# Sums across the 32-partition groups: one fp32 matmul, or a rounded part and a rest in one fp32r matmul

## The chip, the cores and the metric

The kernel runs on one core of a Trainium2 chip, in one launch. The metric is device time in microseconds (us). PE is the matrix engine, PEld its weight load, DVE the vector engine, ACT the scalar engine, POOL the GpSimd engine, SP the engine that issues most DMAs. SBUF is the on-chip memory of 128 partitions, PSUM the memory that PE writes.

## The reference

A transformer block with adaptive layer norms, cut to what matters:

```python
mod = (silu(c) @ w_mod).reshape(1, 6, 1, 576)        # sa, ca, ga, sb, cb, gb
h = layernorm(x) * (1 + ca) + sa                     # x: 1 x 2048 x 576
x = x + ga * A(h)
h = layernorm(x) * (1 + cb) + sb
x = x + gb * B(h)

def A(x):                                            # attention, 32 heads of 128, 16 key/value heads
    q = x @ wq
    k, v = last 512 rows of k_cache, v_cache
    p = softmax(q @ k.T * 128 ** -0.5)               # over 512 keys
    return (p @ v) @ wo

def B(x):                                            # feed-forward, 4608 wide
    return (relu(x @ W_gate) * (x @ W_up)) @ W_down
```

All inputs and the output are fp32. The softmax of A needs, for each query, a maximum over 512 keys and a sum over 512 keys.

## The kernel before, in words

Attention is done in 128 units. A unit is one head and one block of 512 queries, and takes the keys as rows: the scores of a unit stand in PSUM as keys x queries, in two halves of 2 x 128 keys (`s_half`, tiles `s`). So maximum and sum over the keys go across the partitions.

Almost all matrix products are in fp32r, the reduced fp32 form that PE takes in one pass. To keep the precision, an operand is split into a rounded part `hi` (an fp32r copy) and the rest `lo` (value minus `hi`), and a product is three matmuls: hi by hi, hi by lo, lo by hi. ACT makes the `hi` copies and POOL the `lo` subtractions. In a unit POOL does two additions for the sum over the keys (`ks`, L548), two subtractions `lo` for the probabilities (L539, 128 x 1024 each), one for the output (`olo`, L573), and in many units one for a weight (L182) or for a later stage (L818, L855, L863, L865).

The maximum of a unit goes in three steps. DVE takes the maxima of blocks of 32 partitions, with a transpose inside (L460, tile `t4`). `max_pre` takes the maximum over the four key tiles (L468, into PSUM) and multiplies it by `mask` (L469), so that each group of 32 partitions ("quadrant") holds its own values in its own of four column groups of 16, and zeros in the others. Then `spread` on PE multiplies these 64 columns by `quad`, a 128 x 128 matrix of ones where two partitions have the same place in their quadrant. That copies the four quadrants' values to all partitions. `max_bc` takes the maximum of the four (L498) and transposes it back to rows (L513). The sum of the unit before rides along: `sum_pre` writes the 32-blocks' sums into 16 more columns (L475, tile `t5`), the same matmul adds the four quadrants, and `sum_inv` takes the reciprocal (L488). The matmul (L483) has thus 80 columns, is in fp32, and shows as two records a time in the profile.

The order of the engines is written out by hand: Tile is told to keep the program's order on PE, DVE, ACT and POOL, and each engine runs its own queue in that order. For unit u it is:

- `s_half` twice, `max_pre(u)`, `sum_pre(u - 1)`
- `qproj(u + 1)`: 14 matmuls on PE for the next unit's queries (L383)
- `spread(u)`, `max_bc(u)`
- a piece of the output projection, 12 matmuls of 288 columns (L584)
- `pv_half(u - 1, 0)`: probabilities by values (L557 to L559)
- `exp_half(u, 0)` and `(u, 1)`: DVE subtracts the maximum (L530), ACT takes the exponential (L532) and the `hi` copy (L519)
- the rest of `pv`, another piece, and at the end `lo_half` twice on POOL (L539)

Between these lie the steps of a schedule (weights' loads and splits, layer norms, preparations for the next stage), each due at a time in tenths of a unit. In the first four units and the last (`by_pe`) the maximum is subtracted on PE; there `max_bc` splits the maxima with an fp32r copy `rh` on DVE (L505 to L508). After the last unit a `spread` with the last sums alone runs inside the feed-forward stage (`last_unit`).

Of the kernel before, what the change touches and what calls it, by code (L numbers as in the profile page):

```python
# [33 lines left out]
def kernel(  # L34
# [13 lines left out]
    nc = tc.nc  # L48
# [3 lines left out]
    cp = ctx.enter_context(tc.tile_pool(name="cp", bufs=1))  # L52
# [7 lines left out]
    op = ctx.enter_context(tc.tile_pool(name="op", bufs=3))  # L60
# [13 lines left out]
    mhalf = cp.tile([P, 4], F32, name="mhalf")  # L74
# [11 lines left out]
    mask = cp.tile([P, 4], F32, name="mask")  # L86
# [8 lines left out]
    nc.vector.tensor_scalar(minus, intc, 0.0, -1.0, op0=ALU.is_equal, op1=ALU.mult)  # L95


    cT = cp.tile([P, 5], F32, name="cT")
    nc.sync.dma_start(cT, c)
    acc = []  # L100
    accp = [res.tile([P, 2, D], F32, tag=f"accp{i}", name=f"acc{i}") for i in range(S // (2 * P))]
# [5 lines left out]
            nc.sync.dma_start(acc[i], x[i * P:(i + 1) * P, :])  # L107


    sT = cp.tile([P, 5], F32, name="sT")  # L110
# [5 lines left out]
    msum = {}  # L116

    steps_done = {}

# [43 lines left out]
    def mod_col(j, plus):  # L163
        m = msum[j]
        assert steps_done[j] == (3 if j == 1 else 5)
        if j < 3:
            mod_pad(j)
        ps = psM.tile([P, 512], F32, tag="mm", name=f"mps{j}")
        for t in range(5):
            nc.tensor.matmul(ps[:, t:t + 1], m[:, t * P:(t + 1) * P], ones[:, 0:1], start=True, stop=True)  # L170
        r = cp.tile([P, 5], F32, name=f"mcol{j}")
# [236 lines left out]
    NU = HKV * NQB * 2  # L408
# [33 lines left out]
    st_, t4, t5, pt, hi_, lo_, bc, rb, rinv, ks_, pvps, done, o, bps = ({} for _ in range(14))  # L442

    def by_pe(u):
        return u < PE0 or u >= NU - PE1
# [16 lines left out]
                                axis=AX.X, op=ALU.max, apply_transpose=True)  # L462

    def max_pre(u):
        t5[u] = sp.tile([P, 5, 16], F32, tag="t5", name=f"t5_{u}", bufs=1)
        bps[u] = psM.tile([P, 512], F32, tag="mm", name=f"qm{u}")
        t = bps[u][:, 128:144]
        nc.vector.tensor_reduce(t, t4.pop(u).rearrange("p k b -> p b k"), axis=AX.X, op=ALU.max)  # L468
        nc.vector.tensor_tensor(t5[u][:, 0:4, :], mask[:, :, None].to_broadcast([P, 4, 16]),  # L469
                                t[:, None, :].to_broadcast([P, 4, 16]), op=ALU.mult)  # L470

    def sum_pre(u):
        if u + 1 == NU:
            t5[NU] = sp.tile([P, 5, 16], F32, tag="t5", name=f"t5_{NU}", bufs=1)
        nc.vector.tensor_reduce(t5[u + 1][:, 4, :],  # L475
                                ks_.pop(u).rearrange("p (b j) -> p b j", j=32),
                                axis=AX.X, op=ALU.add, apply_transpose=True)

    def spread(u):
        a, b = (0 if u < NU else 4), (5 if u else 4)  # L480
        if u == NU:
            bps[u] = psM.tile([P, 512], F32, tag="mm", name=f"qm{u}")
        nc.tensor.matmul(bps[u][:, a * 16:b * 16], quad,  # L483
                         t5.pop(u)[:, a:b, :].rearrange("p a b -> p (a b)"), start=True, stop=True)

    def sum_inv(u):
        r = rinv[u] = sp.tile([P, 16], F32, tag="ri", name=f"ri{u}", bufs=1)
        nc.vector.reciprocal(r, bps[u + 1][:, 64:80])  # L488

    def sum_bc(u):  # L490
        r = rinv.pop(u)
# [2 lines left out]
                            r[:, :, None].to_broadcast([P, 16, 32]))  # L494

    def max_bc(u):
        r = sp.tile([P, 16], F32, tag="r", name=f"r{u}", bufs=1)
        nc.vector.tensor_reduce(r, bps[u][:, :64].rearrange("p (a b) -> p b a", a=4), axis=AX.X, op=ALU.max)  # L498
        if u:
            sum_inv(u - 1)  # L500
        m = bp.tile([P, 512], F32, tag="bc", name=f"mb{u}")
        if by_pe(u):
            rh = sp.tile([P, 16], F32R, tag="rh", name=f"rh{u}", bufs=1)
            rr = sp.tile([P, 16, 2], F32, tag="rr", name=f"rr{u}", bufs=1)
            nc.vector.tensor_copy(rh, r)  # L505
# [657 lines left out]
    e = 10 * NU  # L1163
# [460 lines left out]
```

## Time and profile before

| | |
|---|---|
| runs, median | 2932.51 us (2930.28 to 2934.88, 3 runs) |
| the profiled execution | 2927.97 us, its span 2926.2 us, mean granted PE clock 0.996 |
| PE busy | 2854.1 us, 98% of the span |
| DVE busy | 2220.3 us, 76% |
| POOL busy | 2110.1 us, 72% |
| ACT busy | 1432.2 us, 49% |
| first and last crossing matmul (L483) | at 42.3 us and at 1651.8 us |

In a row of the profile stand the line of the kernel, the engine, the operation, the tile written and those read, the shapes, and the count; then the busy time and the mean length of one in ns, and the idle time of the engine in front of them with what ended it. A timeline's row has the start, the length, the engine, the line, and the count of like instructions that are merged in it; in square brackets stands the idle time in front and what ended it. In a line's own view the three numbers are the shortest, the median and the longest in ns, and then the first and the last start in us. In the table by stretches stand the length, the busy times of PE, PEld, DVE, ACT and POOL with their counts, the granted clock, the DMA share and GB/s.

### The profile page before, as it was taken

How to read it: one execution, taken by the hardware profiler on the slowest of the kernel's cores; microseconds unless marked ns; L12 is line 12 of the kernel's file. 1: busy time of each engine (PE TensorE's matmuls, PEld its weight loads, DVE VectorE, ACT ScalarE, POOL GpSimd, SP SyncE). 2: the span in 40 equal slices, each digit the busy share in tenths (PEclk: the TensorE clock that was granted, in tenths of full speed). 3: DMA queues.
4: the chain of work that ended last, by engine and by line, in shares of the span. 5: the costliest groups of instructions: out<-in, count | busy, mean ns of one | idle time of the engine just before them, and what ended most of it. 6: DMA issues, size and time to landing. Idle time of an engine off the chain costs nothing. (4 is left out here: it accounts for less than half of the span.)

```text
span 2926.2 us, 41388 instructions
## 1 busy us (share of the span) xinstructions
PE 2854.1 (98%) x15214; PEld 2483.7 (85%) x15214; DVE 2220.3 (76%) x3082; ACT 1432.2 (49%) x2029; POOL 2110.1 (72%) x1564
## 2 busy tenths in 40 slices
PE   6799999999999999999999999999999999999999
PEld 5588888888888888888888788888888888888888
DVE  7878888788878888777889677677777466666666
ACT  4566666666666666666656343333333122222221
POOL 5588888888888889876778666777777356656553
PEclk9999999999999999999999999999999999999999
DMA  4011222222223223322244456666666944444442
GB/s 151 22 45 55 82 94 84 67 98 93 92 83 107 90 63 133 101 70 85 65 145 135 135 214 223 229 230 222 225 227 243 331 160 153 151 152 153 158 151 104
DMA packets 162698, 396.44 MB, mean 135 GB/s; under 512 B 14912, under 2 KB 61760, under 8 KB 162496
## 3 DMA queue, kind: packets, MB, share of 16 engines
q1 hardware_dynamic: 131472, 282.15, 29.9%
q10 hardware_dynamic: 31024, 111.65, 9.8%
q8 instruction: 120, 1.97, 0.3%
q14 instruction: 82, 0.67, 0.1%
HBM read 268.73 MB, written 153.32 MB: 144 GB/s over the span
## 5 line engine op out<-in xcount | busy, mean ns | idle before, releaser
L539 POOL TENSOR_TENSOR lo<-p,hi 128x1024 fp32r<-128x1024 f32 x256 | 609.7, 2403 | 1.1 <-ACT hi L519 1.1
L548 POOL TENSOR_TENSOR ks<-ks,p 128x512 f32<-128x512 f32 x256 | 343.7, 1343 | 271.1 <-ACT p L532 206.6
L460 DVE TRANSPOSE_TENSOR_REDUCE t<-s 128x32 f32<-128x1024 f32 x256 | 316.7, 1243 | 137.4 <-PE s L457 125.9
L929 PE MATMUL gu<-hop_B,wop 128*128 128x512 f32 (+1 forms) x1512 | 378.2, 393 | 0.0
L929 PE MATMUL gu<-hop_T,wop 128*128 128x512 f32 (+1 forms) x1260 | 320.5, 394 | 1.9 <-DMA wop<-wk_P 1.9
L383 PE MATMUL qps<-hTa,wA 128*128 128x512 f32 x1288 | 311.7, 393 | 9.4 <-ACT lfa L365 8.9
L929 PEld LDWEIGHTS gu<-hop_B,wop 128*128 128x128 f32 (+1 forms) x1512 | 275.8, 188 | 52.1 <-ACT lflh L914 0.9
L584 PE MATMUL wo<-woga,ohi 128*128 128x288 f32 x1472 | 305.9, 301 | 1.5 <-DVE lfa L363 1.5
L383 PEld LDWEIGHTS qps<-hTa,wA 128*128 128x128 f32 x1288 | 244.2, 190 | 61.7 <-ACT lfa L365 8.2
L530 DVE TENSOR_TENSOR p<-s,mb 128x1024 f32<-128x1024 f32 x246 | 290.1, 1218 | 4.1
L519 ACT CAST hi<-p 128x1024 fp32r<-128x1024 f32 x256 | 268.9, 1050 | 7.1
L584 PE MATMUL md<-wogb,hhi 128*128 128x288 f32 x1280 | 261.8, 297 | 9.6 <-DVE acc L595 8.7
L929 PEld LDWEIGHTS gu<-hop_T,wop 128*128 128x128 f32 (+1 forms) x1260 | 228.1, 188 | 43.8 <-DMA wop<-wk_P 2.1
L532 ACT ACTIVATE p<-p 128x1024 f32<-128x1024 f32 x246 | 259.9, 1056 | 8.0 <-DVE p L530 7.9
L584 PEld LDWEIGHTS wo<-woga,ohi 128*128 128x128 f32 x1472 | 238.7, 188 | 9.1 <-issue 1.9
L435 ACT ACTIVATE qhi<-qps 128x512 fp32r<-128x512 f32 x128 | 76.5, 597 | 340.8 <-PE qps L383 340.8
L595 DVE TENSOR_TENSOR acc<-md,acc 128x576 f32<-128x576 f32 x160 | 120.5, 754 | 152.6 <-PE md L584 151.5
L584 PEld LDWEIGHTS md<-wogb,hhi 128*128 128x128 f32 x1280 | 212.8, 188 | 24.8 <-DVE acc L595 12.7
L1039 DVE TENSOR_TENSOR acc<-st_P,acc 128x576 f32<-128x576 f32 x160 | 120.9, 756 | 133.8 <-PE st_P L1030 133.8
L584 PE MATMUL wo<-woga,olo 128*128 128x288 f32 x736 | 216.9, 295 | 0.3 <-POOL olo L573 0.2
L584 PE MATMUL md<-wogb,hlo 128*128 128x288 f32 x640 | 188.9, 295 | 0.0
L573 POOL TENSOR_TENSOR olo<-rb,ohi 128x512 fp32r<-128x512 f32 x128 | 166.6, 1302 | 23.7 <-ACT ohi L569 23.2
(249 smaller groups left out, 7093.2 us busy)
## 6 DMA issues: line engine op xcount, KB each, us to landing
wop<-wk_P SPq DMA_DIRECT2D x133, 640.0 KB
wk_P<-wop ACTq DMA_DIRECT2D x119, 640.0 KB
wr<-wlay SPq DMA_DIRECT2D x68, 384.0 KB
rogb<-wd SPq DMA_DIRECT2D x68, 288.0 KB
againq<-akq SPq DMA_DIRECT2D x18, 640.0 KB
rwA<-wq SPq DMA_DIRECT2D x32, 320.0 KB
wlay<-wg SPq DMA_DIRECT2D x36, 256.0 KB
roga<-wo SPq DMA_DIRECT2D x32, 288.0 KB
```

The lines of the kernel that those rows point to most:

```text
L383: return [lambda i=i, a=a, b=b: nc.tensor.matmul(ps, a, b, start=(i == 0), stop=(i == n - 1)) for i, (a, b) in enumerate(ops)]
L460: nc.vector.tensor_reduce(t4[u][:, 2 * h:2 * h + 2, :].rearrange("p k b -> p (k b)"), t.rearrange("p k (b j) -> p (k b) j", j=32), axis=AX ...
L519: nc.scalar.copy(hi_[u, h], pt[u, h])
L530: nc.vector.tensor_tensor(p, t, bc[u][:, None, :].to_broadcast([P, 2, 512]), op=ALU.subtract)
L532: nc.scalar.activation(p, p, AF.Exp, bias=0.0, scale=1.0)
L539: nc.gpsimd.tensor_sub(lo_[u, h], pt[u, h], hi_[u, h].bitcast(F32))
L548: nc.gpsimd.tensor_tensor(ks_[u], ks_[u], p[:, j, :], op=ALU.add)
L573: nc.gpsimd.tensor_sub(olo[u], o.pop(u), ohi[u].bitcast(F32))
L584: nc.tensor.matmul(ps[:, half, :H2], a[:, sl], w[b][:, cs], start=(n == 0 and seed is None), stop=(n == 5), skip_group_check=seed is not None)
L595: nc.vector.tensor_tensor(av, ps[:, :, :H2], av, op=ALU.add)
L929: nc.tensor.matmul(ps, a, c, start=s not in ("P2", "P3") and i == 0, stop=i == len(ops) - 1, skip_group_check=True)
L1039: nc.vector.tensor_tensor(t, ps[:, :, :H2], t, op=ALU.add)
```

## The change

The 80 columns are no longer multiplied in fp32. `max_pre` and `sum_pre` write a tile `te`. A new step `cut(u)`, after them and before `qproj(u + 1)`, makes on DVE a rounded fp32r copy of it and the rest (value minus copy), side by side in `t5`. `spread` multiplies both, 160 columns, by `quad` (now fp32r) in one fp32r matmul. A new step `spread_add` on DVE adds the two halves again in PSUM, then takes the maximum of the four quadrants and the reciprocal; the maximum now stays in PSUM. In a unit that makes one copy, one subtraction and one reduce more on DVE. To make room, small constants share one tile `small`, and some tags are shared.

```diff
-    quad = cp.tile([P, P], F32, name="quad")
+    quad = cp.tile([P, P], F32R, name="quad")
...
     def max_pre(u):
-        t5[u] = sp.tile([P, 5, 16], F32, tag="t5", name=f"t5_{u}", bufs=1)
         bps[u] = psM.tile([P, 512], F32, tag="mm", name=f"qm{u}")
-        t = bps[u][:, 128:144]
+        t = bps[u][:, 160:176]
         nc.vector.tensor_reduce(t, t4.pop(u).rearrange("p k b -> p b k"), axis=AX.X, op=ALU.max)
-        nc.vector.tensor_tensor(t5[u][:, 0:4, :], mask[:, :, None].to_broadcast([P, 4, 16]),
+        te[u] = sp.tile([P, 5, 16], F32, tag="t4", name=f"te{u}", bufs=1)
+        nc.vector.tensor_tensor(te[u][:, 0:4, :], mask[:, :, None].to_broadcast([P, 4, 16]),
                                 t[:, None, :].to_broadcast([P, 4, 16]), op=ALU.mult)
...
+    def groups(u):
+        return 0 if u < NU else 4, 5 if u else 4
+
+    def cut(u):
+        a, b = groups(u)
+        e = te.pop(u)[:, a:b, :]
+        t5[u] = sp.tile([P, 2, 5, 16], F32R, tag="t5", name=f"t5_{u}", bufs=1)
+        hi, lo = (t5[u][:, i, a:b, :] for i in range(2))
+        nc.vector.tensor_copy(hi, e)
+        nc.vector.tensor_sub(lo, e, hi.bitcast(F32))
+
     def spread(u):
-        a, b = (0 if u < NU else 4), (5 if u else 4)
+        a, b = groups(u)
         if u == NU:
             bps[u] = psM.tile([P, 512], F32, tag="mm", name=f"qm{u}")
-        nc.tensor.matmul(bps[u][:, a * 16:b * 16], quad,
-                         t5.pop(u)[:, a:b, :].rearrange("p a b -> p (a b)"), start=True, stop=True)
-
-    def sum_inv(u):
-        r = rinv[u] = sp.tile([P, 16], F32, tag="ri", name=f"ri{u}", bufs=1)
-        nc.vector.reciprocal(r, bps[u + 1][:, 64:80])
+        n = (b - a) * 16
+        nc.tensor.matmul(bps[u][:, :2 * n].rearrange("p (s n) -> p s n", s=2), quad,
+                         t5.pop(u)[:, :, a:b, :].rearrange("p s a b -> p s (a b)"), start=True, stop=True)
+
+    def spread_add(u):
+        a, b = groups(u)
+        n = (b - a) * 16
+        sx = bps[u][:, 176:176 + n]
+        nc.vector.tensor_reduce(sx, bps[u][:, :2 * n].rearrange("p (s n) -> p n s", s=2), axis=AX.X, op=ALU.add)
+        if u < NU:
+            r = bps[u][:, 256:272]
+            nc.vector.tensor_reduce(r, sx[:, :64].rearrange("p (a b) -> p b a", a=4), axis=AX.X, op=ALU.max)
+        if u:
+            ri = rinv[u - 1] = sp.tile([P, 16], F32, tag="ri", name=f"ri{u - 1}", bufs=1)
+            nc.vector.reciprocal(ri, sx[:, n - 16:])
+        return r if u < NU else None
...
     def max_bc(u):
-        r = sp.tile([P, 16], F32, tag="r", name=f"r{u}", bufs=1)
-        nc.vector.tensor_reduce(r, bps[u][:, :64].rearrange("p (a b) -> p b a", a=4), axis=AX.X, op=ALU.max)
-        if u:
-            sum_inv(u - 1)
+        r = spread_add(u)
...
     def last_unit():
+        cut(NU)
         spread(NU)
-        sum_inv(NU - 1)
+        spread_add(NU)
...
         max_pre(u)
         if u:
             sum_pre(u - 1)
+        cut(u)
         run(u, 1)
         if u + 1 < NU:
             qproj(u + 1, 0, 14)
```

More of the change, by code (lines that the diff above doesn't have):

```diff
@@ L73 @@
     nc.vector.tensor_scalar(ident, ident, 0.0, None, op0=ALU.is_equal)
-    mhalf = cp.tile([P, 4], F32, name="mhalf")
+    small = cp.tile([P, 33], F32, name="small")
+    mhalf, mask, sT = small[:, :4], small[:, 4:8], small[:, 8:13]
     nc.vector.memset(mhalf, -0.5)
@@ L85 @@
     inta = bp.tile([P, 4], I32, tag="bc", name="inta")
-    mask = cp.tile([P, 4], F32, name="mask")
     nc.gpsimd.iota(inta, pattern=[[-32, 4]], base=0, channel_multiplier=1)
@@ L95 @@
     nc.vector.tensor_scalar(minus, intc, 0.0, -1.0, op0=ALU.is_equal, op1=ALU.mult)
-    cT = cp.tile([P, 5], F32, name="cT")
+    cT = sp.tile([P, 5], F32, tag="t4", name="cT", bufs=1)
     nc.sync.dma_start(cT, c)
@@ L107, in load_x @@
             nc.sync.dma_start(acc[i], x[i * P:(i + 1) * P, :])
-    sT = cp.tile([P, 5], F32, name="sT")
     nc.scalar.activation(sT, cT, AF.Exp, bias=0.0, scale=-1.0)
@@ L114 @@
     nc.vector.tensor_tensor(sT, sT, cT, op=ALU.mult)
-    msum = {}
+    msum, cols = {}, []
     steps_done = {}
@@ L170, in mod_col @@
             nc.tensor.matmul(ps[:, t:t + 1], m[:, t * P:(t + 1) * P], ones[:, 0:1], start=True, stop=True)
-        r = cp.tile([P, 5], F32, name=f"mcol{j}")
+        r = small[:, 13 + 5 * len(cols):18 + 5 * len(cols)]
+        cols.append(j)
         def done():
@@ L440, in q_lo @@
                                        op0=ALU.mult, op1=ALU.subtract)
-    st_, t4, t5, pt, hi_, lo_, bc, rb, rinv, ks_, pvps, done, o, bps = ({} for _ in range(14))
+    te, st_, t4, t5, pt, hi_, lo_, bc, rb, rinv, ks_, pvps, done, o, bps = ({} for _ in range(15))
     def by_pe(u):
@@ L473, in sum_pre @@
         if u + 1 == NU:
-            t5[NU] = sp.tile([P, 5, 16], F32, tag="t5", name=f"t5_{NU}", bufs=1)
-        nc.vector.tensor_reduce(t5[u + 1][:, 4, :],
-                                ks_.pop(u).rearrange("p (b j) -> p b j", j=32),
+            te[NU] = sp.tile([P, 5, 16], F32, tag="t4", name=f"te{NU}", bufs=1)
+        nc.vector.tensor_reduce(te[u + 1][:, 4, :], ks_.pop(u).rearrange("p (b j) -> p b j", j=32),
                                 axis=AX.X, op=ALU.add, apply_transpose=True)
+    def groups(u):
[7 more added lines that the diff above has]
+        nc.vector.tensor_sub(lo, e, hi.bitcast(F32))
     def spread(u):
-        a, b = (0 if u < NU else 4), (5 if u else 4)
+        a, b = groups(u)
         if u == NU:
             bps[u] = psM.tile([P, 512], F32, tag="mm", name=f"qm{u}")
-        nc.tensor.matmul(bps[u][:, a * 16:b * 16], quad,
-                         t5.pop(u)[:, a:b, :].rearrange("p a b -> p (a b)"), start=True, stop=True)
-    def sum_inv(u):
-        r = rinv[u] = sp.tile([P, 16], F32, tag="ri", name=f"ri{u}", bufs=1)
-        nc.vector.reciprocal(r, bps[u + 1][:, 64:80])
+        n = (b - a) * 16
[13 more added lines that the diff above has]
+        return r if u < NU else None
     def sum_bc(u):
@@ L496, in max_bc @@
     def max_bc(u):
-        r = sp.tile([P, 16], F32, tag="r", name=f"r{u}", bufs=1)
-        nc.vector.tensor_reduce(r, bps[u][:, :64].rearrange("p (a b) -> p b a", a=4), axis=AX.X, op=ALU.max)
-        if u:
-            sum_inv(u - 1)
+        r = spread_add(u)
         m = bp.tile([P, 512], F32, tag="bc", name=f"mb{u}")
         if by_pe(u):
-            rh = sp.tile([P, 16], F32R, tag="rh", name=f"rh{u}", bufs=1)
-            rr = sp.tile([P, 16, 2], F32, tag="rr", name=f"rr{u}", bufs=1)
+            rh = sp.tile([P, 16], F32R, tag="t5", name=f"rh{u}", bufs=1)
+            rr = sp.tile([P, 16, 2], F32, tag="t4", name=f"rr{u}", bufs=1)
             nc.vector.tensor_copy(rh, r)
```

## Prediction

> **What bounds the kernel now.** I read the page's totals first, then who waits around the matmul that the change replaces, then the order of time of one attention unit, then POOL's rows.
>
> ```profile
> span 2926.2 us, 41388 instructions
> PE 2854.1 (98%) x15214; PEld 2483.7 (85%) x15214; DVE 2220.3 (76%) x3082; ACT 1432.2 (49%) x2029; POOL 2110.1 (72%) x1564
> L539 POOL TENSOR_TENSOR lo<-p,hi 128x1024 fp32r<-128x1024 f32 x256 | 609.7, 2403 | 1.1 <-ACT hi L519 1.1
> ```
>
> PE is busy for 98% of the span, so PE's stream is the limit and anything that holds it back costs in full. The source view of the crossing (L483) says how close it is to doing that already:
>
> ```profile
> L483 PE MATMUL qm<-t,quad x258: 180/272/337, 42.3 to 1651.8; 128*128 128x80 f32 x127, 128*128 128x64 f32 x1, 128*128 128x16 f32 x1
>   DVE t L475: 17.2, 22
> ```
>
> Each of the 129 crossings is two matmul records. PE waited for DVE's operand before 22 of them only, 17.2 us in all; in the others the operand lay ready. Here is that place in one unit, from the timelines of all engines, of DVE and of ACT:
>
> ```profile
> 1256.66 0.22 DVE L498 TENSOR_REDUCE r<-qm 128x16 f32<-128x64 f32 x1 [0.93 <-PE qm L483]
> 1257.66 2.35 DVE L530 TENSOR_TENSOR p<-s,mb 128x1024 f32<-128x1024 f32 x2
> 1258.36 0.64 ACT L593 COPY acc<-wo 128x576 f32<-128x576 f32 x1
> 1259.61 1.05 ACT L532 ACTIVATE p<-p 128x1024 f32<-128x1024 f32 x1
> ...
> 1265.40 4.75 POOL L539 TENSOR_TENSOR lo<-p,hi 128x1024 fp32r<-128x1024 f32 x2
> 1266.31 2.21 PE L383 MATMUL qps<-hTa,againq 128*128 128x512 f32 x9
> 1266.66 0.28 DVE L468 TENSOR_REDUCE qm<-t 128x16 f32<-128x64 f32 x1
> 1266.97 0.22 DVE L469 TENSOR_TENSOR t<-mask,qm 128x64 f32<-128x64 f32 x1
> 1267.11 0.70 DVE L475 TRANSPOSE_TENSOR_REDUCE t<-ks 128x16 f32<-128x512 f32 x1
> 1268.35 0.35 PE L483 MATMUL qm<-t,quad 128*128 128x80 f32 x2
> 1268.50 0.52 PE L584 MATMUL wo<-againo,ohi 128*128 128x288 f32 x2
> 1268.74 0.22 DVE L498 TENSOR_REDUCE r<-qm 128x16 f32<-128x64 f32 x1 [0.93 <-PE qm L483]
> 1268.86 0.29 PE L584 MATMUL wo<-againo,olo 128*128 128x288 f32 x1
> 1268.99 0.43 PE L584 MATMUL wo<-againo,ohi 128*128 128x288 f32 x2
> 1269.25 0.29 PE L584 MATMUL wo<-againo,olo 128*128 128x288 f32 x1
> ```
>
> The operand is complete at 1267.81 and PE comes to it at 1268.35: 0.54 us of slack. L498 to L498 is 12.08 us, one unit. At 1267.81 POOL is inside its two `lo` subtractions, which last until 1270.15. That decides this change.
>
> **The PE part.** Nine 512-column matmuls run from 1266.31 to 1268.35, 0.227 us from start to start; a 288-column one takes 0.13 (1268.86 to 1268.99). On that line 160 columns are 0.08 us. The two old records take 0.15 (1268.35 to 1268.50), and the pair behind them 0.36 (1268.50 to 1268.86) where a later pair takes 0.26 (1268.99 to 1269.25): 0.25 in all. Gain 0.17 us on the path, 129 times: 22 us.
>
> **DVE behind the matmul.** The re-adding reduce (160 in, 80 out, PSUM to PSUM) has no row. Below it stands L498 at 0.22, above it the 0.70 of L475, which reads 512; I take 0.38, L468 with some 96 more elements. With a gap of 0.03 (L468 to L469) the maxima come 0.4 us later. The cover is ACT: the first half of L530 ends near 1258.84, but ACT takes it at 1259.61, since its copies of the output sum (L593) are in front: 0.77 us. Those copies follow PE's piece behind the crossing, so they come 0.17 earlier and leave 0.6 for 0.4. I cost it at nothing; without the cover it would be 0.4 x 129 = 52 us. `r` now stays in PSUM until L513 has read it, so the bank goes on to the next product some 0.9 us later; that product starts behind PE's piece of 12 matmuls (12 x 0.13 = 1.6 us), about when the bank comes free. Nothing, to 0.1 us a unit.
>
> **DVE in front of the matmul.** The cut is a copy that rounds, SBUF to SBUF, then a subtraction of two SBUF operands that waits for the copy. By length they are small: the shortest cast below is 126 ns, the subtraction is L469's 0.22; with a gap 0.38 us, inside the 0.54. But these two kinds of DVE work do not run beside POOL here:
>
> ```profile
> L505 DVE CAST rh<-r x5: 126/935/1543, 43.0 to 1626.5; 128x16 fp32r<-128x16 f32 x5
> 55.06 2.38 POOL L539 TENSOR_TENSOR lo<-p,hi 128x1024 fp32r<-128x1024 f32 x1
> 56.48 1.00 DVE L505 CAST rh<-r 128x16 fp32r<-128x16 f32 x1
> L371 DVE TENSOR_TENSOR hTa<-lfa,hTa x13: 684/692/2879, 26.8 to 132.1; 128x512 fp32r<-128x512 f32 x10, 64x512 fp32r<-64x512 f32 x3
> 80.20 2.69 POOL L548 TENSOR_TENSOR ks<-ks,p 128x512 f32<-128x512 f32 x2 [1.51 <-ACT p L528]
> 80.60 2.58 DVE L367 CAST hTa<-lfa 128x512 fp32r<-128x512 f32 x2
> 82.86 5.32 POOL L539 TENSOR_TENSOR lo<-p,hi 128x1024 fp32r<-128x1024 f32 x2
> 83.10 5.63 DVE L371 TENSOR_TENSOR hTa<-lfa,hTa 128x512 fp32r<-128x512 f32 x2
> ```
>
> The cast of 16 elements took 1.00 us and ended at 57.48, when POOL's subtraction ended (57.44). Two casts and two subtractions in a row took 2.58 and 5.63 us, where one subtraction takes 0.69, and kept pace with four POOL instructions, one DVE instruction behind each. So each such DVE instruction waits for POOL's running instruction, and POOL's next, if it stands ready, goes in between two of them. The Trainium skill's "SBUF — State Buffer", section "Who interferes with whom", states such a rule: a copy in a two-port mode, or an operation with two SBUF inputs, takes a port pair shared with GpSimd as an exclusive lock, and the one that comes first holds it for its whole instruction. The traces agree (1.00 us for that cast); without such a rule the sum would be the 22 us of gain and no more.
>
> So the copy waits for POOL and the subtraction for POOL's next instruction. Which one that is comes from POOL's timeline:
>
> ```profile
> 1258.46 1.30 POOL L573 TENSOR_TENSOR olo<-rb,ohi 128x512 fp32r<-128x512 f32 x1 [0.39 <-ACT ohi L569]
> 1262.78 2.68 POOL L548 TENSOR_TENSOR ks<-ks,p 128x512 f32<-128x512 f32 x2 [3.01 <-ACT p L532]
> 1270.09 1.32 POOL L573 TENSOR_TENSOR olo<-rb,ohi 128x512 fp32r<-128x512 f32 x1
> 1277.48 4.74 POOL L539 TENSOR_TENSOR lo<-p,hi 128x1024 fp32r<-128x1024 f32 x2
> 1282.62 1.30 POOL L573 TENSOR_TENSOR olo<-rb,ohi 128x512 fp32r<-128x512 f32 x1 [0.40 <-ACT ohi L569]
> ...
> 1032.17 2.67 POOL L548 TENSOR_TENSOR ks<-ks,p 128x512 f32<-128x512 f32 x2 [1.10 <-ACT p L532]
> 1034.80 1.57 POOL L182 TENSOR_TENSOR wA<-rwA,wA 128x640 fp32r<-128x640 f32 x1
> 1036.32 4.75 POOL L539 TENSOR_TENSOR lo<-p,hi 128x1024 fp32r<-128x1024 f32 x2
> ```
>
> Count time from a crossing's start: 1268.35, and 12.08 before it 1256.27; 1025.66 for the third unit, if its L548 also starts 6.51 behind the crossing (1262.78 - 1256.27). POOL's work follows ACT, and ACT follows PE's piece behind the crossing, so all of it comes 0.17 earlier. PE sees DVE's result some 0.06 us late, my estimate from the opposite way (L483 ends at 1268.70, L498 starts at 1268.74).
> - Kind A (after 1268.35): the operand is done just after the second `lo` began, that `lo` ends at 13.87 - 0.17 = 13.70, the copy takes 0.13, POOL's next waits for ACT (0.40 idle), so the subtraction follows: 0.03 + 0.22 + 0.06. Next crossing at 14.1, not 12.08: +2.1.
> - Kind B (after 1256.27): the same, but POOL's L573 stands ready (1270.09, before the `lo` ends) and goes between: 13.71 + 0.13 + 1.32 + 0.31 = 15.5: +3.4.
> - Kind C (after 1025.66): a weight's split lies between L548 and L539, the copy meets the first `lo`, which ends at 13.04 - 0.17 = 12.87, the second `lo` goes between (2.40): 12.87 + 0.13 + 2.40 + 0.31 = 15.7: +3.6. With the shorter pieces that stand there in other units it is 3.2; 3.4 on average.
>
> I counted the units from the sixth to the 127th in POOL's timeline: 14 of kind A, 62 of B, 46 of C. Sum: 14 x 2.1 + 62 x 3.4 + 46 x 3.4 = 397 us, the PE gain already in it. The first five units and the last crossing I put at 10 (0 to 20), since POOL stands idle in part of them. Queued behind the waiting subtraction on DVE is only the reduce that needs the matmul anyhow; behind the waiting matmul stands the whole PE stream. No DMA moves. Shared tags and the tile `small` cost nothing: their readers and writers are DVE instructions in order, or long done.
>
> The profiled execution took 2927.97 us, 2 us beyond its span; the median of the runs is 2932.51. 2932 + 397 + 10 gives **3340 us**.
>
> **Rivals.**
> 1. *The subtraction follows the copy at once*, POOL never getting in between. Then A and B cost 2.1, C 12.87 + 0.13 + 0.31 = 13.3, so 1.2: 76 x 2.1 + 46 x 1.2 = 215, plus 5: 3150. Against it stands the 5.63 us pair. Halfway to it: the operand is ready only about 0.03 us after the second `lo` begins (1267.81 against 1265.40 + 2.40); if the copy slips in front, B costs 2.1 as well, and the sum falls by 62 x 1.3 = 80 to 3260.
> 2. *PE's clock drops as well.* In the new rhythm PE stands idle some 3.5 us in each unit of kind B and C, and the trace has this, in the table by stretches (the granted clock is the last but two of the columns):
>
> ```profile
> 41.40:44.80 3.40, 0.47 (x3) 0.30 (x2) 2.70 (x8) 0.00 (x0) 2.51 (x3) 1.00 0.04 13
> 44.80:51.60 6.80, 5.60 (x12) 3.97 (x13) 5.24 (x12) 5.15 (x6) 1.42 (x2) 0.50 0.19 58
> ```
>
> After 3.4 us with 0.47 us of PE work the granted clock was 0.50 for 6.8 us. If such a stretch follows nearly every one of the 108 long gaps and slows the piece in front of ACT's copies (12 x 0.13 = 1.6 us of PE work becomes 3.2, less about 0.5 that is hidden), it adds 108 x 1.1 = 119 us: 3460. If it follows few, it is lost in the range. The Trainium skill's "TensorE: Matmul & The Clock Gate", section "What's actually happening", has the clock halve after one free-running idle window of about 3.4 us; by it a gap of 3.5 us would trip only where it fills a window. The stretch above tripped with 0.47 us of work in it.
> 3. *Faster.* The copy and the subtraction find POOL idle and stay inside the 0.54 us of slack. Then the 22 us stand alone: 2911. It decides at whether the operand is complete outside of L539; for it speaks that POOL idles 3.0 us in a unit (in front of L548), against it that this idle time lies 5 us from the cut in every unit shown, and that both move together with the crossing.
> 4. *No change*: the 0.4 us behind the matmul uncovered in a part of the units while POOL is out of the way; 2932.
>
> **How the numbers follow.** Forecast (with the halfway case) 0.70, rival 1 0.11, rival 2 0.15, rival 3 0.03, rival 4 0.01. The range goes from 3170, above rival 1, to 3470, rival 2; rival 1 and a few per cent beyond rival 2 are outside. A measurement of this kernel tells about 0.2% from no change. Faster 0.03, within it 0.01, slower 0.96.
>
> **What would show it.** In the changed kernel's profile: the cut's two DVE lines with means near 1 and 2 us instead of 0.13 and 0.22; PE idle before the crossing in nearly every unit, released by the subtraction, 2 to 4 us each; the crossing as one record, 129 in all; POOL's own busy time unchanged; units of 14 to 16 us; the time behind 1650 us of before (the feed-forward stage) as long as it was. I am wrong if those two lines show their bare lengths, if the cast alone waits and the subtraction does not (rival 1), or if the loss lies behind the matmul instead of in front.

## The result, and the profile after

The changed kernel takes **3414.92 us** (median of 4 runs, 3407.66 to 3417.75) against 2931.41 in the same comparison: 1.164 times as long, 95% interval 1.162 to 1.166. The forecast was 3340, its range 3170 to 3470. The profiled execution took 3415.74, with a span of 3413.8.

The page of the changed kernel: totals and three of the costliest groups (busy us, mean ns of one | idle time in front, and what ended it); the last row is the old crossing, of the kernel before.

```profile
span 3413.8 us, 41516 instructions
PE 3010.6 (88%) x15085; PEld 2576.6 (75%) x15085; DVE 2674.5 (78%) x3469; ACT 1435.6 (42%) x2029; POOL 2105.0 (62%) x1564
L494 PE MATMUL qm<-t,quad 128*128 128x160 f32 (+1 forms) x129 | 47.5, 368 | 339.3 <-DVE t L487 339.3
L486 DVE CAST t<-te 128x80 fp32r<-128x80 f32 (+1 forms) x129 | 242.0, 1876 | 4.4
L556 POOL TENSOR_TENSOR lo<-p,hi 128x1024 fp32r<-128x1024 f32 x256 | 606.2, 2389 | 0.8 <-ACT hi L536 0.8
L483 PE MATMUL qm<-t,quad 128*128 128x80 f32 (+1 forms) x258 | 46.1, 259 | 7.0 <-DVE t L475 6.1 <-DVE t L469 0.8
```

The crossing is one record, 129 times. PE stands idle in front of it for 339.3 us, all of it until the subtraction of the cut (L487) is done; in front of the old crossing it was 7.0. PE's busy time has grown by 156.5 us, though it has 129 records fewer. 332 us more of this idle time and 156.5 us more of busy time are the 487.6 us by which the span grew, to within 2. POOL's busy time is the same (2105 against 2110), and the `lo` subtraction takes what it took (2389 ns against 2403). The feed-forward stage behind the last crossing is as long as before: 1275.5 us from there to the end of the span (3413.8 - 2138.3), 1274.4 before (2926.2 - 1651.8).

Now both lines of the cut, from the source view (min/median/max ns):

```profile
L486 DVE CAST t<-te x129: 169/1850/7115, 43.8 to 2137.8; 128x80 fp32r<-128x80 f32 x127, 128x64 fp32r<-128x64 f32 x1, 128x16 fp32r<-128x16 f32 x1
L487 DVE TENSOR_TENSOR t<-te,t x129: 177/1227/2319, 44.3 to 2138.1; 128x80 fp32r<-128x80 f32 x127, 128x64 fp32r<-128x64 f32 x1, 128x16 fp32r<-128x16 f32 x1
```

The shortest of each, 0.17 and 0.18 us, have the 16 columns of the last crossing; with 80 columns and POOL idle the two take 0.20 and 0.24 (at 107.12 and 107.35). Their medians are 1.85 and 1.23. Here is where that time goes, in the timelines of POOL, DVE and PE. First a unit of kind A, from its predecessor's crossing on, then one of kind B:

```profile
1775.00 0.34 PE L494 MATMUL qm<-t,quad 128*128 128x160 f32 x1 [1.82 <-DVE t L487]
1784.10 4.72 POOL L556 TENSOR_TENSOR lo<-p,hi 128x1024 fp32r<-128x1024 f32 x2
1786.06 0.71 DVE L475 TRANSPOSE_TENSOR_REDUCE te<-ks 128x16 f32<-128x512 f32 x1
1786.80 2.08 DVE L486 CAST t<-te 128x80 fp32r<-128x80 f32 x1
1788.91 0.24 DVE L487 TENSOR_TENSOR t<-te,t 128x80 fp32r<-128x80 f32 x1
1789.21 0.34 PE L494 MATMUL qm<-t,quad 128*128 128x160 f32 x1 [1.75 <-DVE t L487]
...
1638.62 0.34 PE L494 MATMUL qm<-t,quad 128*128 128x160 f32 x1 [1.68 <-DVE t L487]
1647.72 4.72 POOL L556 TENSOR_TENSOR lo<-p,hi 128x1024 fp32r<-128x1024 f32 x2
1650.37 2.13 DVE L486 CAST t<-te 128x80 fp32r<-128x80 f32 x1
1652.40 1.27 POOL L590 TENSOR_TENSOR olo<-rb,ohi 128x512 fp32r<-128x512 f32 x1
1652.54 1.23 DVE L487 TENSOR_TENSOR t<-te,t 128x80 fp32r<-128x80 f32 x1
1653.82 0.34 PE L494 MATMUL qm<-t,quad 128*128 128x160 f32 x1 [2.78 <-DVE t L487]
```

In the first the cast is ready while the second `lo` runs; `lo` ends at 1788.82, the cast at 1788.88. Nothing of POOL stands ready, the subtraction takes its bare 0.24, and the unit is 14.21 us long. The reduce in front of the cast (L475) reads and writes SBUF too, beside the same `lo`, and takes its 0.71, as before (0.70): not every DVE instruction waits. In the second the cast ends when `lo` does, POOL's L590 goes in between, the subtraction ends when that ends, and the unit is 15.20 us long.

Two things were not in the forecast's sum. The first is the clock. In the table by stretches of the changed kernel (the granted clock is the last but two of the columns):

```profile
50.00:2150.00 2100.00, 1738.45 (x8196) 1462.36 (x8195) 1771.06 (x2344) 1056.92 (x1417) 1292.37 (x806) 0.92 0.21 67
996.00:999.00 3.00, 0.00 (x0) 0.00 (x0) 2.96 (x2) 0.00 (x0) 2.65 (x3) 0.50 0.14 48
999.00:1002.40 3.40, 3.35 (x14) 3.35 (x15) 2.71 (x6) 0.00 (x0) 0.00 (x0) 0.51 0.30 78
1653.80:1657.20 3.40, 3.38 (x15) 3.29 (x16) 2.90 (x6) 0.18 (x1) 0.00 (x0) 0.57 0.05 20
```

Over the attention stage the mean clock is 0.92. The trace's record of the granted clock holds only 1 and 0.5: in this stage 80 stretches at 0.5, of 3.4 us or two or three times that, 341 of the 2100 us. The second and third rows are one such place: PE waits, the clock halves, and the 3.4 us behind the crossing run slow. The last row is the time behind the unit of kind B above, where PE had waited 2.78 us. I counted the 122 units from the sixth to the 127th: a stretch at 0.5 begins during PE's wait, or within 1.7 us behind the crossing, for all 26 waits of over 3 us, for 32 of the 37 of 2.5 to 3, for 10 of the 27 of 2 to 2.5, and for 4 of the 32 shorter ones. The second thing is how long PE waited at the first of the two places:

```profile
990.45 0.45 POOL L880 TENSOR_TENSOR wb_P<-wa_P,wb_P 32x128 fp32r<-32x128 f32 x1
990.87 0.73 POOL L882 TENSOR_TENSOR wa_P<-wa_P,wb_P 128x256 fp32r<-128x256 f32 x1
991.56 4.65 POOL L556 TENSOR_TENSOR lo<-p,hi 128x1024 fp32r<-128x1024 f32 x2
991.60 7.11 DVE L486 CAST t<-te 128x80 fp32r<-128x80 f32 x1
996.18 1.25 POOL L590 TENSOR_TENSOR olo<-rb,ohi 128x512 fp32r<-128x512 f32 x1
997.40 1.25 POOL L182 TENSOR_TENSOR kv<-rkv,kv 128x512 fp32r<-128x512 f32 x1
998.75 0.24 DVE L487 TENSOR_TENSOR t<-te,t 128x80 fp32r<-128x80 f32 x1
```

One cast waited through four POOL instructions in a row, where elsewhere it gets in behind the one that runs. 11 units have a cast of over 4 us like this, 9 of them through four POOL instructions and 2 through three.

### The profile page after: what moved, and what is told of

The parts are those of the page before. It is cut to its first block, busy times and chain, and to the rows that moved or that the text cites. A ratio compares the mean times of both kernels' runs of the same rounds, so it can differ in the third digit from the quotient of the medians.

```text
span 3413.8 us, 41516 instructions
## 1 busy us (share of the span) xinstructions
PE 3010.6 (88%) x15085; PEld 2576.6 (75%) x15085; DVE 2674.5 (78%) x3469; ACT 1435.6 (42%) x2029; POOL 2105.0 (62%) x1564
## 4 chain that ended last, share of the span: by engine, by line
PE 68%; DVE 28%; issue 2%; DMA 1%; ACT 1%; POOL 0%; SPq 0%; ACTq 0%; DVEq 0%; POOLq 0%
PE gu L946 22%; PE wo L601 13%; DVE t L486 7%; PE md L601 7%; DVE t L460 5%; PE st_P L1047 5%; DVE t L487 5%; PE pv L574 4%; PE pv L575 4%; PE pv L576 3%; PE s L457 3%; PE s L456 3%; PE s L455 3%; DVE te L475 2%; DVE wr L752 1%
## 5 line engine op out<-in xcount | busy, mean ns | idle before, releaser
L556 POOL TENSOR_TENSOR lo<-p,hi 128x1024 fp32r<-128x1024 f32 x256 | 606.2, 2389 | 0.8 <-ACT hi L536 0.8
L494 PE MATMUL qm<-t,quad 128*128 128x160 f32 (+1 forms) x129 | 47.5, 368 | 339.3 <-DVE t L487 339.3
L601 PE MATMUL wo<-woga,ohi 128*128 128x288 f32 x1472 | 342.5, 327 | 1.8 <-DVE lfa L363 1.8
L494 PEld LDWEIGHTS qm<-t,quad 128*128 128x128 f32 x129 | 26.2, 203 | 393.5 <-DVE t L487 393.5
L547 DVE TENSOR_TENSOR p<-s,mb 128x1024 f32<-128x1024 f32 x246 | 290.3, 1219 | 4.2
L601 PEld LDWEIGHTS wo<-woga,ohi 128*128 128x128 f32 x1472 | 272.3, 214 | 9.4 <-issue 2.2
L610 ACT COPY acc<-wo 128x576 f32<-128x576 f32 x233 | 148.3, 636 | 308.9 <-PE wo L601 301.7
L590 POOL TENSOR_TENSOR olo<-rb,ohi 128x512 fp32r<-128x512 f32 x128 | 164.2, 1283 | 177.4 <-ACT ohi L586 174.5
L486 DVE CAST t<-te 128x80 fp32r<-128x80 f32 (+1 forms) x129 | 242.0, 1876 | 4.4
L601 PE MATMUL wo<-woga,olo 128*128 128x288 f32 x736 | 240.5, 327 | 0.0
```

What stands on the lines that cost most here:

```text
L486: nc.vector.tensor_copy(hi, e)
L547: nc.vector.tensor_tensor(p, t, bc[u][:, None, :].to_broadcast([P, 2, 512]), op=ALU.subtract)
L556: nc.gpsimd.tensor_sub(lo_[u, h], pt[u, h], hi_[u, h].bitcast(F32))
L601: nc.tensor.matmul(ps[:, half, :H2], a[:, sl], w[b][:, cs], start=(n == 0 and seed is None), stop=(n == 5), skip_group_check=seed is not None)
```

## The experiments

The theory: each of the cut's two DVE instructions, SBUF to SBUF, waits for POOL's running instruction, and POOL's next goes in between. The rivals: the two instructions are late for another reason; only one of them waits; the clock makes the loss.

**The unrounded values in PSUM.** The cut has the same instructions, but both read `te` from the crossing's PSUM bank.

```
-        te[u] = sp.tile([P, 5, 16], F32, tag="t4", ...)
+        te[u] = bps[u][:, 272:352].rearrange("p (a b) -> p a b", a=5)
```

> The changed kernel with te in PSUM (in the crossing's own bank) in place of SBUF: the copy then has a PSUM source, and the subtraction one SBUF operand (the rounded part) in place of two. Same instructions, same count, same order. Theory (each of the two waits because both of its sides, or two inputs, lie in SBUF while POOL works there): the two take about 0.2 to 0.3 us each in every unit, PE waits for them by 0 to 0.2 us a unit, the 22 us of PE gain come back: 2905 to 2945 us. Rival (three more DVE instructions and a chain of waits in front of PE cost the time, wherever the tile lies): stays above 3300 us.

Measured: 3011.29 us (3010.05 to 3016.02), 1.028 times the kernel before, 1.026 to 1.029. From the source view:

```profile
L486 DVE CAST t<-qm x128: 224/242/242, 42.0 to 1703.8; 128x80 fp32r<-128x80 f32 x127, 128x64 fp32r<-128x64 f32 x1
L487 DVE TENSOR_TENSOR t<-qm,t x128: 224/241/242, 42.2 to 1704.1; 128x80 fp32r<-128x80 f32 x127, 128x64 fp32r<-128x64 f32 x1
```

The waits are gone to the last one: 242 ns is the longest cast. So 404 of the 483.5 us hang on where these two instructions read. The Trainium skill's "SBUF — State Buffer", section "Who interferes with whom", names the same condition (two SBUF inputs, or a copy in a two-port mode); 242 ns against 1850 agrees. But 80 us of loss stay, where at most 14 were expected, and the next two runs ask why.

**And the bank set free.** The maxima `r` go to SBUF again, so that the bank is free before the transposition (L530) has read them.

```
-            r = bps[u][:, 256:272]
+            r = sp.tile([P, 16], F32, tag="r", name=f"r{u}", bufs=1)
```

> The kernel with the unrounded values in PSUM (3011 us), and the maxima r written to SBUF again instead of staying in the crossing's PSUM bank. If the next product's first matmul starts late because its bank is held until the transposition has read r (0.26 us in each of some 122 units), 32 us go: 2979 (2970 to 2990). If that product starts late for another reason (its weights, or PE's order), nothing moves: 3011 (3005 to 3016). The wait of the crossing itself, 0.30 us a unit, stays in both cases.

Measured: 2983.05 us, ratio 1.018 (1.016 to 1.019): 28 us less. The timeline around the first matmul of the next product (L574), with the crossing and DVE's transposition ahead of it, of the kernel with `r` in PSUM, then PE alone with `r` in SBUF:

```profile
1346.97 0.34 PE L494 MATMUL qm<-t,quad 128*128 128x160 f32 x1
1348.16 0.65 DVE L530 STREAM_TRANSPOSE mb<-qm 128x512 f32<-128x512 f32 x1
1348.65 0.29 PE L601 MATMUL wo<-ro,olo 128*128 128x288 f32 x1
1348.96 0.47 PE L574 MATMUL pv<-hi,againv 128*128 128x512 f32 x1
```
```profile
1339.56 0.30 PE L601 MATMUL wo<-ro,olo 128*128 128x288 f32 x1
1339.69 0.39 PE L574 MATMUL pv<-hi,againv 128*128 128x512 f32 x1
```

The transposition ends at 1348.81, and the product starts 0.15 us later. Its 0.31 us behind the piece became 0.13, and that matmul 0.47 became 0.39: 0.26 us a unit, as in the theory. What stays is 52 us, and it lies in front of the crossing: from the start of PE's last matmul ahead of it to its own start it is 82.7 us in the sum over the 122 units, before 32.5. DVE there, of the kernel with `r` in SBUF:

```profile
1336.22 0.23 DVE L469 TENSOR_TENSOR qm<-small,qm 128x64 f32<-128x64 f32 x1
1336.55 0.73 DVE L475 TRANSPOSE_TENSOR_REDUCE qm<-ks 128x16 f32<-128x512 f32 x1
1337.31 0.24 DVE L486 CAST t<-qm 128x80 fp32r<-128x80 f32 x1
1337.59 0.24 DVE L487 TENSOR_TENSOR t<-qm,t 128x80 fp32r<-128x80 f32 x1
```

From the start of L469 to the operand it is 1.61 us; before it was 0.84 (1266.97 to 1267.81). The cut is 0.55 of the 0.77. The rest is the move to PSUM itself: the sums' reduce starts 0.33 behind L469 instead of 0.14, and takes 0.73 instead of 0.70. The slack was 0.54, so PE waits 0.23, and a little for the signal.

**The crossing later on PE.** To hide that wait, the crossing stands behind 4 of the 12 matmuls of the piece that followed it.

```
                    n += 1
+                    if mid and half == 0 and n == 4:
+                        mid.pop()()          # spread(u), max_bc(u), q_hi(u + 1)
```

> The kernel with PSUM operands and r in SBUF, and on PE the crossing stands behind the first 4 of the 12 matmuls of the piece that followed it (0.52 us of PE work) instead of in front of them. The operand, 0.30 us late now, is then 0.2 us early. If the two waits are all that is left (0.30 and 0.26 us a unit), PE never waits and keeps the gain of the cheaper crossing: 2915 (2900 to 2935). If the work behind the crossing on DVE and ACT, now 0.5 us later against PE's stream, has no cover left, the wait comes back at the next product or the next scores, up to 0.3 us a unit: 2950 to 2975.

Measured: 2965.36 us, ratio 1.012 (1.010 to 1.013), 18 us less than in front of the piece, and inside the range of the second forecast. The cover is used up: ACT waits for DVE's L547 in 108 units, 37.5 us in all, where it was 9 units and 10.7 us. And PE still waits for the subtraction, 29.1 us in 27 waits.

**PE's part alone.** The kernel before, with maxima and sums written already rounded, one fp32r matmul of 80 columns, the rest left out, no cut.

```
-    quad = cp.tile([P, P], F32, name="quad")
+    quad = cp.tile([P, P], F32R, name="quad")
-        t5[u] = sp.tile([P, 5, 16], F32, tag="t5", ...)
+        t5[u] = sp.tile([P, 5, 16], F32R, tag="t5", ...)
```

> The kernel before with only PE's part: the maxima and sums are written to SBUF already rounded to fp32r, the rest is left out, and the crossing is one fp32r matmul of 80 columns instead of two f32 records. No cut, no re-adding (the output is less exact). By the prediction's terms one record of 0.04 us takes the place of two of 0.15 and the 0.10 of the slow pair behind them goes too: 0.21 x 129 = 27, so 2904 (2898 to 2912). If the gain is the 0.03 us that is seen in the kernel with PSUM operands, 4 us: 2927 (2922 to 2932).

Measured: 2921.02 us against 2930.85, ratio 0.9960 (0.9948 to 0.9973). PE's timeline:

```profile
1271.07 0.20 PE L484 MATMUL qm<-t,quad 128*128 128x80 f32 x1
1271.10 0.50 PE L585 MATMUL wo<-againo,ohi 128*128 128x288 f32 x2
1271.44 0.29 PE L585 MATMUL wo<-againo,olo 128*128 128x288 f32 x1
```

From the crossing to the third matmul behind it are 0.37 us, before 0.51 (1268.35 to 1268.86). So PE's part, here with 80 columns, is worth 0.14 us on PE and 10 us in the kernel, between the two expected values (2904 and 2927) and by far the smaller side of this trade. The sums are less exact in this kernel, so it is no full replacement.

**One of the two instructions at a time.** In the first run the subtraction is replaced by setting the rest to zero, in the second the cast by setting the rounded part to zero.

```
-        nc.vector.tensor_sub(lo, e, hi.bitcast(F32))
+        nc.vector.memset(lo.bitcast(F32), 0.0)
```
```
-        nc.vector.tensor_copy(hi, e)
+        nc.vector.memset(hi.bitcast(F32), 0.0)
```

> The changed kernel, with the rest not computed (a memset of its half of the tile to 0 in place of the subtraction; the sums and maxima are then rounded). The copy stays SBUF to SBUF. Theory (copy waits for POOL's running instruction, POOL's next goes in between, subtraction waits for that one): the second wait goes. Units of kind A and B pay about 1.9 us over 12.08, kind C 1.1: 76 x 1.9 + 46 x 1.1 = 195, about 3130 us, with up to 60 more where PE's clock halves. Rival 1 of the prediction (both waits end together): the time stays within 60 us of 3415.

> The changed kernel with the rounding copy replaced by setting the rounded part to zero; the subtraction of the two SBUF operands stays (the rounded parts are left out). If a waiting DVE instruction gets in behind POOL's running one, and it was the second of the two that cost the next POOL instruction, one of them alone waits once: about the 3215 us of the kernel with the copy alone (3190 to 3240). If the subtraction were the one that POOL's queue holds back, whatever stands in front of it, it stays near 3380 to 3415.

Measured: 3215.02 us with the cast alone, 25 above the most that was expected, and 3220.16 with the subtraction alone, as expected. The source views of the two:

```profile
L486 DVE CAST t<-te x129: 169/2059/7131, 43.7 to 1936.1; 128x80 fp32r<-128x80 f32 x127, 128x64 fp32r<-128x64 f32 x1, 128x16 fp32r<-128x16 f32 x1
```
```profile
L487 DVE TENSOR_TENSOR t<-te,t x129: 174/2002/7016, 42.5 to 1938.3; 128x80 fp32r<-128x80 f32 x127, 128x64 fp32r<-128x64 f32 x1, 128x16 fp32r<-128x16 f32 x1
```

Either kind takes the same 2.0 us when it comes first; the one that comes second costs another 195 to 200 us. The memset in the place of the other does not wait (125 ns at most), so it is the cast and the subtraction that do.

**Shorter POOL instructions.** The `lo` subtractions are cut into halves of 512 elements.

```
-        nc.gpsimd.tensor_sub(lo_[u, h], pt[u, h], hi_[u, h].bitcast(F32))
+        for j in range(2):
+            nc.gpsimd.tensor_sub(lo_[u, h][:, j, :], pt[u, h][:, j, :], hi_[u, h][:, j, :].bitcast(F32))
```

> The changed kernel with each of POOL's lo subtractions (128 x 1024) issued as two of 128 x 512. Same work, shorter instructions. Theory (DVE waits for whole POOL instructions): the copy waits 0.6 us on average and the subtraction one piece of about 1.25: the next crossing some 13.7 us behind the last, 1.6 over 12.08, about 3130 to 3200 us. Rival (DVE waits until POOL has no work, or the two share the memory by rate): 3380 to 3450 us.

Measured: 3238.69 us, 39 above the theory's range and far below the rival's.

```profile
L557 POOL TENSOR_TENSOR lo<-p,hi 128x512 fp32r<-128x512 f32 x512 | 643.8, 1289 | 0.7 <-ACT hi L536 0.7
L486 DVE CAST t<-te x129: 168/865/7419, 43.8 to 1960.9; 128x80 fp32r<-128x80 f32 x127, 128x64 fp32r<-128x64 f32 x1, 128x16 fp32r<-128x16 f32 x1
L487 DVE TENSOR_TENSOR t<-te,t x129: 176/1225/1360, 44.3 to 1961.1; 128x80 fp32r<-128x80 f32 x127, 128x64 fp32r<-128x64 f32 x1, 128x16 fp32r<-128x16 f32 x1
```

The cast's median fell from 1.85 to 0.87 us, the longest subtraction from 2.32 to 1.36. So the wait goes by whole POOL instructions, whatever their length. The casts that are passed over stay as long as they were (7.4) and hold the mean cast at 1.14 us.

**PE kept busy.** 8 of the 14 matmuls of each query projection from unit 6 on are done twice: 976 more matmuls, 222 us of PE work at 0.227 each.

```
+        if u > 5:
+            w, h = wqs[unit(u)[2]], hT[unit(u)[1]]
+            for i in range(8):
+                nc.tensor.matmul(qst[u][0], w[:, i // 2 + 5 * (i % 2), :], h[i // 2], ...)
```

> The changed kernel with PE work added in front of the crossing: from unit 6 on, the next unit's projection begins with 8 of its matmuls done once more into the same bank and then overwritten (8 x 0.227 = 1.8 us a unit, 220 us of PE work in all). PE stands idle there for 2.45 us in the median, so the work should fit in the wait. If the halved PE clock after such gaps is part of the loss, as much as the forecast missed: the mean granted clock returns to 0.98 or more and the time falls to 3310 to 3390 us. If the clock costs nothing: 3415 to 3450. If PE were the limit in spite of its gaps: 3415 + 220 = 3635 us.

Measured: 3362.09 us. With 222 us more of work the kernel is 53 us shorter. The attention stage in the table by stretches:

```profile
50.00:2100.00 2050.00, 1878.23 (x9197) 1567.36 (x9197) 1798.90 (x2349) 1056.37 (x1420) 1298.26 (x808) 0.97 0.21 68
```

The mean clock rose from 0.92 to 0.97, and PE's busy time in the whole kernel by 137 us only (3010.6 to 3148.0). So its other work got some 85 us faster. The cut did not get cheaper:

```profile
L490 DVE CAST t<-te x129: 169/2044/7139, 43.3 to 2083.1; 128x80 fp32r<-128x80 f32 x127, 128x64 fp32r<-128x64 f32 x1, 128x16 fp32r<-128x16 f32 x1
```

The cast's median is 2.04 us where it was 1.85, and cast and subtraction together take 419 us in the kernel where they took 398. So the slow clock costs the changed kernel at least 53 us. This part is shown by the runs, its full size is not: at 0.97 some of it is still there.

**The 32-row instruction.** In the 11 units with the long casts, L880, a subtraction of 32 partitions, stands 1 to 3 us ahead in POOL's queue, and POOL works on without a gap until the cut comes. L880 runs 14 times; in the other 3 units the cut comes 9 to 11 us behind it, POOL has been idle for 2.9 to 4.3 us in between, and the cast takes 2.1 to 2.4 us. First it is left out, then it covers all 128 partitions.

```
-            nc.gpsimd.tensor_sub(hi[0:32, 256:], a[0:32, 256:], hi[0:32, 256:].bitcast(F32))
```
```
-            nc.gpsimd.tensor_sub(hi[0:32, 256:], a[0:32, 256:], hi[0:32, 256:].bitcast(F32))
+            nc.gpsimd.tensor_sub(hi[:, 256:], a[:, 256:], hi[:, 256:].bitcast(F32))
```

> The changed kernel without the 32-partition subtraction on POOL that stands in front of the split of a later weight's 256 columns (14 instructions of some 1 us; the rest of that tail is left out). If it is what lets POOL pass the cut over for three or four instructions in 11 units (copies of 4.1 to 7.1 us), those copies fall to 2 us or less and some 35 us go, clock included: 3380 (3365 to 3395). If not, the long copies stay and the time falls by no more than POOL's own 14 us: 3402 to 3416.

> The changed kernel with the subtraction of a later weight's tail over all 128 partitions instead of 32, at the same place, with the same 128 columns (the other 96 rows of that tail come out without their rounded part). If the long waits of the cut in 11 units come from an instruction that covers 32 partitions only, they vanish as when it is left out: 3382 (3370 to 3392). If they come from one more short instruction at that place of POOL's queue, they stay: 3415 (3405 to 3422).

Measured: 3380.76 us without it, 3382.88 with 128 partitions, against 3415.74 in the changed kernel's profiled run. The cast and the wider instruction in the second:

```profile
L486 DVE CAST t<-te x129: 168/1504/2428, 42.6 to 2106.2; 128x80 fp32r<-128x80 f32 x127, 128x64 fp32r<-128x64 f32 x1, 128x16 fp32r<-128x16 f32 x1
L880 POOL TENSOR_TENSOR wb_P<-wa_P,wb_P x14: 450/462/472, 955.4 to 1586.1; 128x128 fp32r<-128x128 f32 x14
```

No cast is longer than 2.43 us any more, and 33 to 35 us go. POOL's instruction stands at the same place and takes the same 0.46 us; only the number of partitions differs. (The first expectation called it 1 us long; it is 0.45.) Why an instruction of 32 rows makes the cut wait through three or four of POOL's instructions stays open.

**Two versions that keep exact sums.** Both write the maxima rounded, without a rest (every exponential and the sum use the same rounded maximum), and cut only the 16 sums, which stand in PSUM. In the first the rounding copy is on ACT and the sums' reduce comes first; in the second all of it is on DVE in the old order.

```
+            es[u + 1] = bps[u + 1][:, 256:272]            # PSUM
+        nc.vector.tensor_reduce(es[u + 1], ks_.pop(u)..., op=ALU.add, apply_transpose=True)
+        nc.scalar.copy(t5[u + 1][:, 4, :], es[u + 1])     # second version: nc.vector.tensor_copy
+        nc.vector.tensor_sub(t5[u][:, 5, :], es[u], t5[u][:, 4, :].bitcast(F32))
```

> A version of the kernel before that takes PE's part and no step that waits for POOL: the maxima cross once, already rounded (the same rounded maximum goes into the exponentials and, through them, into their sums, so the quotient keeps its exactness); only the 16 sums are cut, the rounding copy on ACT, which stands idle some 3 us in front of the crossing, the rest on DVE from a PSUM operand. The crossing is one fp32r matmul of 96 columns, a short reduce (about 0.22 us, as the reduce of 64) adds the two parts of the sums behind the maxima. DVE's chain in front of the crossing is longer by one instruction of 0.24 us, inside the 0.54 us of slack; the maxima's transposition comes 0.25 us later, inside the 0.77 us. If so, the gain of the kernel with rounded values alone stays but for 16 more columns (0.01 us): 2922 (2917 to 2928). If ACT's copy comes late or the reduce is not hidden, up to 0.3 us a unit comes back: up to 2958.

> The version with rounded maxima and cut sums, but the sums' rounding copy is on DVE from PSUM too, and DVE's order is the old one (maxima, sums, copy, rest). In the version with ACT's copy DVE waits 0.26 us in each unit for that copy and PE comes to the crossing 0.33 us behind the last matmul in front of it instead of 0.26. On DVE the copy costs its own 0.14 to 0.17 us instead of the wait, so the chain is about 0.1 us shorter a unit; if the chain is what is left, 9 to 12 us go: 2928 (2922 to 2933). If the loss lies in the added reduce behind the crossing, nothing moves: 2938 (2934 to 2942).

Measured: 2938.05 us with ACT's copy, ratio 1.0018 (1.0009 to 1.0027), 16 above what was expected, and 2961.81 with DVE's, 1.010 (1.008 to 1.012). Neither beats the kernel before, and the second expectation was wrong in its sign. DVE in the second:

```profile
1276.01 0.22 DVE L467 TENSOR_TENSOR t<-mask,qm 128x64 fp32r<-128x64 f32 x1
1276.33 0.73 DVE L484 TRANSPOSE_TENSOR_REDUCE qm<-ks 128x16 f32<-128x512 f32 x1
1277.10 0.17 DVE L486 CAST t<-qm 128x16 fp32r<-128x16 f32 x1
1277.30 0.17 DVE L476 TENSOR_TENSOR t<-qm,t 128x16 fp32r<-128x16 f32 x1
```

The chain from L467 to the operand is 1.46 us, 0.62 more than before, over the slack of 0.54. Cutting 16 columns instead of 80 saves little: an instruction of 16 takes 0.17, one of 80 0.24. In the first version a plain unit is even a little shorter than before (12.00 against 12.08 us) and the loss sits in longer units: PE waits for the rest of the sums 16.4 us in 21 of them, where it waited 6.1 in 5 before. Which step of DVE is late there stays open.

## Why the prediction was right, and where it was off

The mechanism, its place and its sign held: the loss is PE's wait for the two cut instructions, and 404 of the 483.5 us go when they no longer read SBUF alone (3414.92 to 3011.29). The size is in part luck. The sum's 407 us are some 429 of waiting less 22 of gain on PE. Measured were 332 us of waiting, 97 less, and PE's busy time grew by 156.5 where it was to fall by 22. Two errors of opposite sign leave 3415 inside the range, nearer to rival 2 (3460) than to the forecast. By the steps:

- **PE's slack.** "22 of them only, 17.2 us in all" adds up the waits of PE and of its weight load. PE itself waited 5 times for L475, 6.1 us, so it was even closer to never waiting.
- **PE's part, 0.17 us.** With 80 columns it was 0.14 where PE runs through, and 10 us in the kernel; the prediction's own terms give 0.21 and 27 for that. With the change's 160 columns, behind a wait, the third matmul comes 0.48 us behind the crossing (1775.00 to 1775.48), 0.03 earlier than before.
- **The re-adding reduce, 0.38 us, hidden.** It took 0.333 (the median of L501). With the cut out of POOL's way and `r` in SBUF, ACT waited for L547 10.7 us in 9 units, before 7.9 in 7 (there L530), so it is hidden.
- **`r` in PSUM, "nothing, to 0.1 us a unit".** Too low: with PE's stream nearly full it cost 0.26 us a unit, 28 us in all (3011.29 to 2983.05). The bank came free later than the piece's 1.6 us: L530 ends 1.84 us behind the crossing (1346.97 to 1348.81).
- **The cut's bare length of 0.38 "inside the 0.54".** Too short: 0.13 was the cast of 16 columns. With 80 and POOL idle it is 0.51 from the end of the reduce (107.08 to 107.59), just inside. From PSUM it is 0.55 with the gaps, with the reduce's later start 0.77, and no longer inside.
- **Kind A, 14.1 us.** 14.21 in the unit shown. **Kind B, 15.5.** 15.20: the subtraction ends 0.1 us behind POOL's L590, where the forecast had it 0.25 behind and the cast's 0.13 in front. **The counts** were off: the subtraction waited for a second POOL instruction (over 0.6 us) in 83 of the 122 units counted, not in 108. The kinds' own sums would give the cast a mean of some 2.0 and the subtraction of some 1.8; "means near 1 and 2 us" does not follow from them, and measured were 1.88 and 1.21. The 122 units together are 470 us longer than before, the slow clock included, where the sum had 397; the longest is 19.24 us, not 16.
- **The clock (rival 2, 119 us, chance 0.15).** This is the term that was missing from the forecast's sum. Its condition, a stretch at 0.5 behind nearly every one of 108 long waits, was met in 72 of the 122 units. It cost 53 us at the least (PE kept busy); 170, half of the 341 us at 0.5, is my estimate of the most, and the growth of PE's busy time lies between. The forecast took it into the range and not into the sum. The Trainium skill's "TensorE: Matmul & The Clock Gate", section "What's actually happening", has the clock halve after an idle window of about 3.4 us. The place shown, where PE waited 6.8 us, agrees with it. But 32 of the 37 waits of 2.5 to 3 us were followed by a halved stretch too, and they cannot fill such a window, so the prediction's reading that a gap must fill it does not hold here.
- **Not foreseen at all:** the 11 casts that POOL passed over, 33 to 35 us with their share of the clock.

Fewer and shorter second waits than forecast, against the clock and the 11 casts: that is how 3340 became 3415. Rival 1 is ruled out by kind B's timeline, where POOL's L590 goes in between, and by the single instructions: the second one to come adds 195 to 200 us. Rivals 3 and 4 are ruled out by the first row of the cut.

## What to carry to other kernels

A small DVE cast from SBUF to SBUF, or a subtraction of two SBUF operands, is priced by what POOL is running when it comes: look at POOL's timeline at that moment, and count POOL instructions, not columns. Here a reduce with one SBUF operand and a memset did not wait. Two waiting instructions in a row cost two of POOL's if POOL's next is ready. Reading the operand from PSUM takes the wait away, but look at what the bank then holds up and at the slack, which here was 0.54 us against a chain of 0.77. When a wait is put in front of a busy PE, add what the clock takes from the work behind it: here waits of 2.5 us and more, once a unit, nearly always brought a stretch at half the clock.

## What the runs showed of the hardware that was not expected

- A waiting DVE instruction normally gets in behind POOL's running one (2.1 us for the cast). Behind a POOL instruction of 32 partitions, with POOL busy without a gap since, it waited through three or four (4.1 to 7.1 us, 11 times); with 128 partitions in the same 0.46 us it did not (2.43 at most).
- The clock halved behind waits of PE well under 3.4 us: 32 of 37 waits of 2.5 to 3 us, 10 of 27 of 2 to 2.5.
- More work made the kernel faster: 222 us of added matmuls, 53 us less time, the mean clock of the attention stage 0.97 instead of 0.92.
- Moving a 16-column result of DVE from SBUF to PSUM made the reduce start 0.19 us later behind the instruction ahead of it (0.33 against 0.14); in the version with DVE's copy, where the instruction ahead still writes SBUF, it is 0.32.
